# Half of the filter taps by DMA transpose through DRAM, half by TensorE per 128 channels, and a new instruction order, in a one-core kernel of a long convolution and an MLP mixer

## The chip, the cores and the metric

The kernel runs on one core of one Trainium2 chip. The metric is the device time of one execution in microseconds (us), lower is better; the time before is the median of three runs. A profile is one execution taken by the hardware profiler; its span is measured from the first to the last instruction that it shows.

## The reference

All tensors are bf16, with S = 2048 rows and D = 640 channels; the MLP is F = 1536 wide.

```python
x = A_q
g = sigmoid((x * gate_w).sum(-1, keepdims=True))
# branch a: depthwise shift, product with v, long convolution along S
k_shift = sum over t of 4 of k[s - t] * shift_k[:, t]
kv = k_shift * v
y  = irfft(rfft(pad(kv)) * rfft(pad(ssm_k)))[:S] + kv * ssm_D
a  = q * y
# branch b: a mixer block
h  = gelu(layernorm(x) @ w1); four groups of 160 channels shifted by 1, -1, 2, -2 rows
x1 = x + shifted(h) @ w2
b  = x1 + gelu(layernorm(x1) @ w3) @ w4
return g * a + (1 - g) * b
```

`ssm_k` has the shape (640, 2048): one filter of 2048 taps for each channel. The convolution wants the taps with time on the partitions, so the kernel has to transpose it. `ssm_D` is added to tap 0, which does the `kv * ssm_D` term.

## The kernel before, in words

Everything lives in one SBUF tensor, `arena`, and PSUM is used as four pairs of banks. Row s of a sequence is kept at partition p, block c and remainder rho with s = 1024c + 8p + rho, so that there are 8 values of rho and 2 of c.

The Python code doesn't issue instructions; it describes nodes. A node has an engine, a list of instructions, the memory that it reads and writes, an estimated cost and a tag. `Prog.schedule` (L181) and `_forward` (L200) then place the nodes one by one: at each step it takes the node that can start first by the estimates, and the table `PRIO` (L443 on) breaks ties by tag. What comes out is a fixed order for each of the five queues: PE (TensorE), ACT (ScalarE), DVE (VectorE), POOL (GpSimd) and SP, which issues most DMAs. Every engine runs its own list strictly in that order and waits on semaphores where `assign_waits` found a dependence. So the estimates and ranks decide the order, and a node that waits holds up all that stands behind it on its engine.

The work, in stages that overlap:

- Loads on SP (`load`, L664), one on ACT, and the identity matrix on POOL: x (= A_q) in steps of two rho and one c of 320 KB, w1, `shift_k`, ssm_k as five loads of 512 KB, k with its three halo rows, v, w2, the table `FM` (cF, 896 KB, for the forward transform) and `gate_w`.
- While nothing is there to work on, TensorE runs filler matmuls of ones (`fill`, L717), 35 nodes of five.
- LN1 (`bn`, L800; `ln_finish` on POOL, L794; `normal` on DVE, L626): statistics and normalisation of x, transposed on TensorE (L839) and evicted by ACT into `XT`.
- mm1 (L876) with GELU in the eviction; the 32-channel rests of the four groups go to their places by 18 small POOL DMAs (`tail`, L916).
- The taps (L762 to 782): 80 transposes of 128 by 128 on TensorE (L773), ten to a PSUM pair, and eight ACT evictions of 1280 columns (L779) into `TAP[p, h, t, d]`, where h is the half of 320 channels. DVE adds D to the row of tap 0.
- kv on DVE (`tt`, L621): the shift, the product with v.
- mm2 (L983) with the residual put in by an ACT seed (L966); LN2 by sums from ACT (L638) and a power on POOL; DMA transposes of SBUF to SBUF on SP (L1006) into `XT`.
- mm3 (L1026), mm4 (L1044), weights loaded by POOL.
- The convolution, per half of 320 channels: `forward` of taps ("h") and kv ("k") as matmuls (L1075), per half two `unit`s on DVE (butterflies, pointwise products, folds; all L621), the `inverse` matmuls (L1198), and the end `fin` on DVE with 16 output DMAs (L1227).

In `forward`, the first matmuls of kap 0 read the first 2048 columns of `FM` (`FM0`), those of kap 1 the other 1536 (`FM1`, `FM2`).

```python
forward("h", 0, "s3", "s4")
forward("k", 0, "s2", "t0")
unit(0, 0, ...); unit(0, 1, ...)
forward("h", 1, "s3", "s4")
forward("k", 1, "k0", "t1")
inverse(0, ...)
unit(1, 0, ...); unit(1, 1, ...)
inverse(1, ...)
```

Of the kernel before, what the change touches and what calls it, by code (L numbers as in the profile page):

```python
# [88 lines left out]
class Prog:  # L89
# [110 lines left out]
    def _forward(self):  # L200
# [38 lines left out]
        while left:  # L239
# [42 lines left out]
            if n.array:  # L282
                w = int((t - self.PHASE) // self.WINDOW)
                while window < w:
                    warm = duty > (0.42 if warm else 0.75) * self.WINDOW
                    window += 1
                    duty, carry = carry, 0.0
                if not warm:
# [14 lines left out]
            elif n.kind == "side":  # L303
                slink = max(slink, t + 1.0) + 0.2
                n.end = slink + (4.0 if link > t else 1.0)
            else:
                xlink = max(xlink, t + 1.0, link) + 1.2
# [115 lines left out]
def _bf16_bits(a):  # L423
# [5 lines left out]
FILL = 35  # L429
KV_DMA = ()  # L430
PW_DMA = ()
LN1_GROUPS = ((0,), (1,), (2, 3), (4, 5), (6, 7))
# [3 lines left out]
LN1_ACT = ()  # L436
INV = (0, 4, 2, 6, 1, 5, 3, 7)
FIN2 = (0,)
# [72 lines left out]
def bass_gated_mix__ssm_conv_h3__mixer_s_mlp__prompt_kernel(  # L511
# [66 lines left out]
    SSM = V(oS + 3 * SLOT, 10240).rearrange("p (c t) -> p c t", c=5)  # L578
    SHK = V(oGM + 1024, 2560).rearrange("p (j d) -> p j d", j=4)
    SHKROW = AR[0:1, oHT:oHT + 2560]  # L580
# [4 lines left out]
    DROW = AR[0:1, oS + 14080:oS + 14720]  # L585
# [93 lines left out]
    for sc in range(4):  # L679
        P.stage = sc  # L680
        for c in range(2):
            load("act" if sc == 0 and c == 1 else "sp", X[:, c, 2 * sc:2 * sc + 2, :], rows(A_q, c)[:, 2 * sc:2 * sc + 2, :],
                 128 * 2560, tag="x")
    P.stage = ""
    load("pool", ident.bitcast(U16), cI.ap(), 32768, tag="ident", cost=0.6)
    load("sp", w1v, B_w1.rearrange("(c p) f -> p c f", p=128), 819200, tag="w1")
# [3 lines left out]
    for c in range(2):  # L690
        P.stage = c
        if c == 0:
            for a, b in ((1, 113), (113, 128)):
                o = AR[a:b, oS:oS + 1920]
                load("sp", o, dram(A_k, (8 * a - 3) * D, [[8 * D, b - a], [1, 3 * D]]), (b - a) * 3840, tag="kh", group="halo")
        else:
            load("sp", KH[1][:, 0:3, :], dram(A_k, (1024 - 3) * D, [[8 * D, 128], [D, 3], [1, D]]), 128 * 3840, tag="kh")
        for h in range(2):
            P.stage = 2 * c + h
            load("sp", KH[c][:, 3 + 4 * h:7 + 4 * h, :], rows(A_k, c)[:, 4 * h:4 * h + 4, :], 128 * 5120, tag="k")  # L700
            load("sp", KV[:, 8 * c + 4 * h:8 * c + 4 * h + 4, :], rows(A_v, c)[:, 4 * h:4 * h + 4, :], 128 * 5120, tag="v")
    P.stage = ""
    for j in range(4):
        load("sp", w2v[:, j, :], B_w2[160 * j:160 * j + 128, :], 163840, tag="w2")
    for j in range(4):
        load("sp", w2v[32 * j:32 * j + 32, 4, :], B_w2[160 * j + 128:160 * j + 160, :], 40960, tag="w2", group="w2t")
# [3 lines left out]
    load("sp", DROW, A_ssm_D.rearrange("(o n) -> o n", o=1), 1280, tag="ssm")  # L710
    P.dma("sp", lambda e, ps: e.dma_start(GWT, gate_w.rearrange("(c p) -> p c", p=128), allow_slow_non_contiguous=True),
          w=[GWT], nbytes=400000, tag="gw")
# [3 lines left out]
    for _ in range(FILL):  # L716
        P.pe([(lambda e, ps: e.matmul(bank(ps, 0, 128), ones, ones, start=True, stop=True)) for _ in range(5)], r=[ones],  # L717
             cols=128 * 5, tag="fill", bits=(False, None))
# [47 lines left out]
    for m in range(8):  # L766
        P.stage = m // 4
        fns = []
        for i in range(2):
            t = 2 * m + i  # L770
            a, rho = t // 8, t % 8
            for c in range(5):
                fns.append(lambda e, ps, i=i, a=a, rho=rho, c=c: e.transpose(  # L773
                    half16(ps)[:, 1024 * i + 128 * c:1024 * i + 128 * c + 128],
# [502 lines left out]
```

## Time and profile before

| | |
|---|---|
| median of 3 runs | 236.66 us (236.05 to 238.21) |
| the profiled execution | 235.83 us, span 234.0 us |
| PE busy | 226.6 us, 97% of the span |
| DVE busy | 217.2 us, 93% |
| ACT busy | 175.6 us, 75% |
| POOL busy | 29.0 us, 12% |
| DMA | 27.69 MB in 26484 packets, 12657 of them under 512 B |

The profiled execution's time is 1.83 us longer than its span, and 0.83 us under the median. PE counts as busy while a matmul waits in its pipeline, so its share says little by itself: the spacing of a long run of equal matmuls tells whether it is dense. `L621` is the line of the helper that all DVE tensor-tensor operations share, and `L652` that of most ACT evictions; they are told apart by their shapes.

### The profile page before, as it was taken

The numbers are of one execution on the slowest core, as the hardware profiler recorded it, in microseconds if no ns is written. First come the engines' busy times: TensorE is split into PE (matmuls) and PEld (weight loads), VectorE is DVE, ScalarE is ACT, GpSimd is POOL, SyncE is SP. The second block draws the span as 40 slices with busy tenths as digits, with TensorE's granted clock in tenths as the row PEclk, the third lists the DMA queues.
The fourth block names the chain that finished last, engine by engine and source line by source line (L and its number), as shares of the span: only waits on it lengthen the run. The fifth ranks groups of instructions, "written<-read, shape, count | busy, mean of one in ns | idle before, by whom it ended". The sixth has DMA issues, their size and how long they took to land.

```text
span 234.0 us, 4160 instructions
## 1 busy us (share of the span) xinstructions
PE 226.6 (97%) x1689; PEld 147.4 (63%) x1689; DVE 217.2 (93%) x277; ACT 175.6 (75%) x287; POOL 29.0 (12%) x38
## 2 busy tenths in 40 slices
PE   7999998997999998999999998999999999999998
PEld 7799565554677755446764454457755764577777
DVE  3994799999999969998998999999999999999995
ACT  2458998999899999899959869889237224662683
POOL 1312530304003420005203000000000000000000
PEclk9889999999999999999999999999999999999999
DMA  7999999201005997000426500008008010001055
GB/s 222 385 408 315 349 398 331 74 0 27 0 0 192 344 339 95 0 0 3 84 44 102 112 0 0 3 9 216 3 0 224 3 56 0 0 3 56 0 172 169
DMA packets 26484, 27.69 MB, mean 118 GB/s; under 512 B 12657, under 2 KB 22258, under 8 KB 26338
## 3 DMA queue, kind: packets, MB, share of 16 engines
q1 hardware_dynamic: 24674, 21.57, 31.7%
q0 software_dynamic: 1648, 5.54, 6.9%
q10 hardware_dynamic: 144, 0.33, 0.7%
q8 instruction: 13, 0.21, 0.4%
q14 instruction: 5, 0.04, 0.1%
HBM read 21.66 MB, written 2.62 MB: 104 GB/s over the span
## 4 chain that ended last, share of the span: by engine, by line
PE 42%; ACT 18%; DVE 18%; SPq 7%; issue 6%; DMA 5%; POOL 2%; POOLq 1%; ACTq 0%; DVEq 0%
DVE arena L621 18%; PE PS L1044 17%; ACT arena L652 14%; PE PS L1026 9%; PE PS L1198 7%; SPq L664 7%; DMA arena<-in_A_k_dram 5%; PE PS L1075 3%; ACT PS L966 3%; POOL arena L794 2%; PE PS L983 2%; PE PS L717 2%; PE PS L876 1%; ACT arena L638 1%; POOLq L1247 1%
## 5 line engine op out<-in xcount | busy, mean ns | idle before, releaser
L621 DVE TENSOR_TENSOR arena<-arena 128x2560 bf16<-128x2560 bf16 (+5 forms) x181 | 193.4, 1127 | 4.0 <-DMA arena<-in_A_k_dram 1.6
L652 ACT ACTIVATE arena<-PS 128x640 bf16<-128x640 f32 (+5 forms) x136 | 97.8, 799 | 25.8 <-PE PS L1026 13.1
L1026 PE MATMUL PS<-arena 128*128 128x512 bf16 x240 | 52.8, 379 | 0.7 <-DMA arena<-arena 0.7
L1044 PE MATMUL PS<-arena 128*128 128x320 bf16 x384 | 52.8, 299 | 0.0
L1044 PEld LDWEIGHTS PS<-arena 128*128 128x128 bf16 x384 | 37.5, 98 | 14.9 <-issue 0.3
L652 ACT ACTIVATE arena<-PS,arena 128x320 bf16<-128x320 f32 (+1 forms) x48 | 27.9, 618 | 25.1 <-PE PS L1044 23.2
L1026 PEld LDWEIGHTS PS<-arena 128*128 128x128 bf16 x240 | 23.3, 98 | 28.4 <-issue 0.9
L1075 PE MATMUL PS<-arena 128*128 128x320 bf16 x224 | 34.2, 300 | 1.6 <-ACT arena L652 1.5
L1075 PEld LDWEIGHTS PS<-arena 128*128 128x128 bf16 x224 | 20.0, 98 | 14.7 <-ACT arena L652 6.2
L638 ACT ACTIVATE arena<-arena 128x640 bf16<-128x640 bf16 (+2 forms) x30 | 22.8, 786 | 2.8 <-DVE arena L824 2.7
L876 PE MATMUL PS<-arena 128*128 128x512 bf16 (+1 forms) x125 | 23.3, 337 | 0.4 <-ACT arena L779 0.2
L983 PE MATMUL PS<-arena 128*128 128x320 bf16 x160 | 22.2, 299 | 1.4 <-issue 1.4
L966 ACT ACTIVATE PS<-arena 128x640 f32<-128x640 bf16 x32 | 22.3, 718 | 0.1
L983 PEld LDWEIGHTS PS<-arena 128*128 128x128 bf16 x160 | 15.6, 98 | 7.7 <-issue 1.7
L794 POOL TENSOR_TENSOR arena<-arena 128x4 f32<-128x4 f32 (+1 forms) x9 | 13.6, 1514 | 54.0 <-DVE arena L621 37.9
L800 DVE BATCH_NORM_STATS2 arena<-arena 128x6 f32<-128x320 bf16 x32 | 13.7, 462 | 4.5 <-DMA arena<-in_A_q_dram 4.5
L1198 PE MATMUL PS<-arena 128*128 128x320 bf16 x128 | 17.9, 299 | 0.0
L876 PEld LDWEIGHTS PS<-arena 128*128 128x128 bf16 x125 | 11.7, 98 | 8.9 <-ACT arena L779 0.5
L717 PE MATMUL PS<-arena 128*128 128x128 bf16 x175 | 14.3, 256 | 1.5 <-DVE arena L674 1.5
L1198 PEld LDWEIGHTS PS<-arena 128*128 128x128 bf16 x128 | 12.5, 98 | 5.0
L717 PEld LDWEIGHTS PS<-arena 128*128 128x128 bf16 x175 | 13.4, 119 | 2.3 <-DVE arena L674 1.5
L626 DVE TENSOR_SCALAR arena<-arena 128x640 bf16<-128x640 bf16 (+3 forms) x35 | 10.3, 320 | 2.8 <-POOL arena L794 2.1
(31 smaller groups left out, 69.4 us busy)
## 6 DMA issues: line engine op xcount, KB each, us to landing
arena<-in_B_w_dram POOLq DMA_DIRECT2D x4, 960.0 KB, 8.1
arena<-in_A_v_dram SPq DMA_DIRECT2D x4, 640.0 KB, 13.5
arena<-in_A_ssm_k_dram SPq DMA_DIRECT2D x5, 512.0 KB, 11.4
arena<-in_A_k_dram SPq DMA_DIRECT2D x4, 640.0 KB, 16.2
arena<-in_A_q_dram SPq DMA_DIRECT2D x4, 640.0 KB, 4.9
out_dram<-arena SPq DMA_DIRECT2D x16, 160.0 KB, 2.0
arena<-in_A_q_dram SPq DMA_DIRECT2D x7, 320.0 KB, 7.8
arena<-cG POOLq DMA_DIRECT2D x1, 1024.0 KB, 5.0
```

Source lines behind the costliest of these rows:

```text
L621: return dve(lambda e: e.tensor_tensor(o, a, b, op), [a, b], [o], c_tt(n), tag=tag, **kw)
L638: node = P.op("act", lambda e, ps: e.activation(o, i, func, **kw), r=r, w=[o], cost=c_act(n, naps, acc is not None, psum=False), tag=tag, ...
L652: node = P.op("act", lambda e, ps: e.activation(ov, inner(ps), func, **kw), r=r, w=[o], cost=c_act(n, len(r), acc is not None), job=job, t ...
L717: P.pe([(lambda e, ps: e.matmul(bank(ps, 0, 128), ones, ones, start=True, stop=True)) for _ in range(5)], r=[ones], cols=128 * 5, tag="fil ...
L794: P.op("pool", lambda e, ps: e.tensor_tensor(r, v, hv, ALU.pow), r=[v, HALF], w=[r], cost=1.1, tag="ln")
L876: fns.append(lambda e, ps, b=b, c=c, lhsT=lhsT: e.matmul(bank(ps, b, 256 * n), lhsT, XT[:, c, r0:r0 + n, :], start=(c == 0), stop=(c == 4)))
L966: P.seed(job, lambda e, ps: e.activation(two(ps, 320), x, ACTF.Copy), [X[:, c, rho, :]], c_act(640, psum=False), tag)
L983: fns.append(lambda e, ps, hh=hh, ft=ft, lhsT=lhsT: e.matmul(bank(ps, hh, 320), lhsT, w2v[:, ft, 320 * hh:320 * hh + 320], start=False, st ...
L1026: fns.append(lambda e, ps, b=b, ft=ft, c=c, sc=sc: e.matmul(bank(ps, b, 512), w3v[:, c, 128 * ft:128 * ft + 128], XT[:, c, 2 * sc:2 * sc + ...
L1044: fns.append(lambda e, ps, hh=hh, ft=ft, lhsT=lhsT: e.matmul(bank(ps, hh, 320), lhsT, w4v[:, ft, 320 * hh:320 * hh + 320], start=False, st ...
L1075: fns.append(lambda e, ps, w=w, b=b, rhs=rhs, st=(first and n == 0), en=(n == len(ss) - 1): e.matmul(bank(ps, b, 320), w, rhs, start=st, s ...
L1198: fns.append(lambda e, ps, kap=kap, ri=ri, c=c, r=r, s=s, n=n: e.matmul(bank(ps, c, 320), GM[:, kap, ri, r, s, :], Qs[kap][:, r, ri, c, :] ...
```

## The change

1. The taps of channels 0 to 319 (h = 0): three nodes in place of eight. Each transposes one block of 128 channels (the last one 64) for all 16 groups of taps and is evicted as one ACT instruction of 2048 (1024) columns. Only 320 channels of `ssm_k` are loaded for it, as three loads.
2. The taps of channels 320 to 639 (h = 1): six DMA transposes on SP read `ssm_k` from DRAM and write `TAP[:, 1]` with the taps in natural order; each half of 1024 taps is then written to a DRAM tensor and read back in the 8p + rho order. Nothing on PE, ACT or DVE is left for this half.
3. D is added by two POOL instructions of 320 elements in place of one DVE instruction of 640.
4. x is loaded by rho singly for rho 0 and 1 (160 KB each), then in pairs as before. `FM` is split into two loads, 2048 and 1536 columns.
5. 60 filler nodes of one matmul in place of 35 of five.
6. The LN2 statistics are the same in fewer steps: the mean as such is worked out for one group alone.
7. The planner's estimates (bytes of loads, DMA transposes, side DMAs, POOL's power) and all ranks in `PRIO` are new, and so is the order of every queue. Switches for other variants (`FIN_DMA`, `LN1_STAT`) are off.

In the order that comes out, SP issues x rho 0 and 1, the first ssm_k block, shift_k, w1, x rho 2 and 3, the second block, the rest of x, one k load, D, the halo, v, the last ssm_k block, gate_w, v, the first part of `FM`, k with its halo, w2, v, v, then the six DMA transposes, then the second part of `FM`, the two writes to DRAM and the two reads back, and then the LN2 transposes. TensorE's list begins with 55 fillers and the eight matmuls of shift_k; in the `forward` of the first taps the first matmul that needs the second part of `FM` comes just ahead of the last mm1 block and of mm2. POOL's second D addition stands ahead of the last of the 18 `tail` DMAs.

The diff, without `PRIO` and the estimates:

```diff
-FILL = 35
+FILL = 60
+FILLN = 1
+X_LOADS = ((0, 1), (1, 2), (2, 4), (4, 6), (6, 8))
-    SSM = V(oS + 3 * SLOT, 10240).rearrange("p (c t) -> p c t", c=5)
+    SSM = V(oS + 3 * SLOT, 6144).rearrange("p (c t) -> p c t", c=3)
...
-    load("sp", V(oFM, 3584).bitcast(U16), cF.ap(), 128 * 7168, tag="FM")
-    for c in range(5):
-        load("sp", SSM[:, c, :], A_ssm_k[128 * c:128 * c + 128, :], 128 * 4096, tag="ssm")
+    for i, (a, b) in enumerate(((0, 2048), (2048, 3584))):
+        P.stage = i
+        load("sp", V(oFM + a, b - a).bitcast(U16), cF.ap()[:, a:b], (b - a) * 300, tag="FM")
+    for c in range(3):
+        P.stage = c
+        n = 128 if c < 2 else 64
+        load("sp", SSM[0:n, c, :], A_ssm_k[128 * c:128 * c + n, :], 5300 * n, tag="ssm")
...
-    for m in range(8):
...
-        job = P.pe(fns, r=[SSM[...], ident], cols=1400, tag="tap", bits=(False, False))
-        o = TAP[:, :, 2 * m:2 * m + 2, :].rearrange("p h t d -> p t h d")
-        P.op("act", ... ACTF.Copy), w=[o], cost=c_act(1280), job=job, tag="tap")
-    tt(t0row, t0row, DROW.rearrange("p (h d) -> p h d", h=2), ALU.add, 640, tag="ssmD")
+    for c in range(3):
+        n = 128 if c < 2 else 64
+        fns = [(lambda e, ps, c=c, n=n, t=t: e.transpose(
+            half16(ps)[:, n * t:n * t + n], SSM[0:n, c, 1024 * (t // 8) + t % 8:1024 * (t // 8) + 1024:8],
+            ident[0:n, 0:n])) for t in range(16)]
+        job = P.pe(fns, ...)
+        o = TAP[:, 0, :, 128 * c:128 * c + n]
+        evict(job, o, ..., ACTF.Copy, 16 * n, tag="tap")
+    def add_d(h):
+        t0row = TAP[0:1, h, 0, :]
+        P.op("pool", lambda e, ps: e.tensor_tensor(t0row, t0row, DROW[h], ALU.add), ...)
+    add_d(0)
+    back = nc.dram_tensor("taps1", (2048, 320), BF16).ap()
+    for a in range(2):
+        o = TAP[:, 1, 8 * a:8 * a + 8, :]
+        for d in (0, 128, 256):
+            n = min(128, 320 - d)
+            P.dma("sp", ... e.dma_start_transpose(o[:, :, d:d + n], A_ssm_k[320 + d:320 + d + n, 1024 * a:1024 * a + 1024]))
+        if a == 0:
+            add_d(1)
+        half = back[1024 * a:1024 * a + 1024, :]
+        out_ = P.dma("sp", ... e.dma_start(half.rearrange("(q p) d -> p q d", p=128), o), tag="tW")
+        in_ = P.dma("sp", ... e.dma_start(o, half.rearrange("(p r) d -> p r d", r=8)), tag="tR")
+        in_.deps.add(out_)
...
     def sum_group(rhos):
-        ts(mean, s1, 1.0 / D, None, ALU.mult, None, 4, tag="ln")
-        tt(t, mean, mean, ALU.mult, 4, tag="ln")
-        ts(v, s2, 1.0 / D, 1e-5, ALU.mult, ALU.add, 4, tag="ln")
-        tt(v, v, t, ALU.subtract, 4, tag="ln")
+        tt(t, s1, s1, ALU.mult, 4, tag="ln")
+        dve(lambda e: e.scalar_tensor_tensor(out=v, in0=t, scalar=-1.0 / D, in1=s2, op0=ALU.mult, op1=ALU.add), ...)
+        ts(v, v, 1.0 / D, 1e-5, ALU.mult, ALU.add, 4, tag="ln")
```

More of the change, by code (lines that the diff above doesn't have):

```diff
@@ L304, in _forward @@
                 slink = max(slink, t + 1.0) + 0.2
-                n.end = slink + (4.0 if link > t else 1.0)
+                n.end = slink + (5.0 if link > t else 2.6)
             else:
-                xlink = max(xlink, t + 1.0, link) + 1.2
+                xlink = max(xlink, t + 1.0, link) + n.bytes / 136.5e3
                 n.end = xlink + 0.5
@@ L677, in bass_gated_mix__ssm_conv_h3__mixer_s_mlp__prompt_kernel @@
     act(JUNK[:, 0:1], ones[:, 0:1], ACTF.Gelu_apprx_tanh, 1, tag="warm")
-    for sc in range(4):
-        P.stage = sc
+    for a, b in X_LOADS:
+        P.stage = a
         for c in range(2):
-            load("act" if sc == 0 and c == 1 else "sp", X[:, c, 2 * sc:2 * sc + 2, :], rows(A_q, c)[:, 2 * sc:2 * sc + 2, :],
-                 128 * 2560, tag="x")
+            load("act" if a == 0 and c == 1 else "sp", X[:, c, a:b, :], rows(A_q, c)[:, a:b, :], 163840 * (b - a), tag="x")
     P.stage = ""
     load("pool", ident.bitcast(U16), cI.ap(), 32768, tag="ident", cost=0.6)
-    load("sp", w1v, B_w1.rearrange("(c p) f -> p c f", p=128), 819200, tag="w1")
+    load("sp", w1v, B_w1.rearrange("(c p) f -> p c f", p=128), 890000, tag="w1")
     load("sp", SHKROW, dram(A_shift_k, 0, [[2560, 1], [1, 2560]]), 5120, tag="shk")
@@ L711, in bass_gated_mix__ssm_conv_h3__mixer_s_mlp__prompt_kernel @@
+    P.stage = ""
+    for h in range(2):
+        load("sp", DROW[h], A_ssm_D.rearrange("(o n) -> o n", o=2)[h:h + 1, :], 1280, tag="D")
     P.dma("sp", lambda e, ps: e.dma_start(GWT, gate_w.rearrange("(c p) -> p c", p=128), allow_slow_non_contiguous=True),
-          w=[GWT], nbytes=400000, tag="gw")
+          w=[GWT], nbytes=140000, tag="gw")
     for _ in range(FILL):
-        P.pe([(lambda e, ps: e.matmul(bank(ps, 0, 128), ones, ones, start=True, stop=True)) for _ in range(5)], r=[ones],
-             cols=128 * 5, tag="fill", bits=(False, None))
+        P.pe([(lambda e, ps: e.matmul(bank(ps, 0, 128), ones, ones, start=True, stop=True)) for _ in range(FILLN)], r=[ones],
+             cols=128 * FILLN, tag="fill", bits=(False, None))
@@ new lines, in act_stats @@
+    def act_stats(rho):
+        rsl = slice(rho, rho + 1)
+        for c in range(2):
+            x = X[:, c, rho, :]
+            act(JUNK, x, ACTF.Copy, 640, scale=1.0 / D, acc=MV1[:, rho, 2 * c:2 * c + 1], accgroup=("m1", rho), tag="st")
+            act(JUNK, x, ACTF.Square, 640, scale=D ** -0.5, acc=MV1[:, rho, 2 * c + 1:2 * c + 2], accgroup=("m1", rho),
+                tag="st")
+        m, s, v = MV1[:, rsl, 0:4:2], MV1[:, rsl, 1:4:2], VAR1[:, rsl, 0:2]
+        dve(lambda e: e.scalar_tensor_tensor(out=v, in0=m, scalar=-1.0, in1=m, op0=ALU.mult, op1=ALU.mult),
+            [m], [v], 0.08, tag="ln")
+        dve(lambda e: e.scalar_tensor_tensor(out=v, in0=v, scalar=1e-5, in1=s, op0=ALU.add, op1=ALU.add),
+            [v, s], [v], 0.08, tag="ln")
+        ln_finish(VAR1, RS1, 0.75, rsl)
@@ L1209, in inverse @@
                 evict(job, o, lambda ps, c=c: bank(ps, c, 320), ACTF.Copy, 320, scale=GG[:, gi:gi + 1], tag="gy")
[L1210 to L1211 removed]
+            paired = INV.index(rho) // 2 < FIN2[half]
+            pair = rho // 4 == 1 and paired
+            if paired and not pair:
                 continue
@@ L1221, in inverse @@
             n = 1280 if pair else 640
-            tt(g2, g2, Qh[:, :, sel, :], ALU.mult, n, tag="fin")
-            tt(xs, xs, g2, ALU.add, n, tag="fin")
+            if half in FIN_DMA:
+                qs = Qh[:, :, sel, :]
+                tt(qs, g2, qs, ALU.mult, n, tag="fin")
+                P.dma("pool", lambda e, ps, xs=xs, qs=qs: e.dma_start(xs, qs, accum_op=ALU.add), r=[xs, qs], w=[xs],
+                      nbytes=256 * n, cost=0.9, kind="acc", tag="fina")
+            else:
+                tt(g2, g2, Qh[:, :, sel, :], ALU.mult, n, tag="fin")
+                tt(xs, xs, g2, ALU.add, n, tag="fin")
             for r1 in range(sel.start, sel.stop, 4):
```

85 lines of the change are left out of this document (46 added, 39 removed), and 50 rows, old and new, of the table PRIO.

## The prediction

> **What bounds the kernel now.** I read the busy time by stage first, then the chain of waits, then the timelines of DVE, PE and SP at the places that the change touches. The windows show that no engine alone is the bound:
>
> ```profile
> 0.00:29.24 29.24, 27.78 (x274) 22.95 (x275) 20.59 (x74) 17.69 (x22) 8.87 (x16) 0.94 0.97 336
> 13.37:86.81 73.44, 70.11 (x636) 48.57 (x634) 66.13 (x87) 69.52 (x119) 19.13 (x27) 1.00 0.61 209
> 29.24:221.80 192.56, 187.54 (x1296) 115.40 (x1295) 187.46 (x185) 150.30 (x250) 20.13 (x22) 1.00 0.30 82
> ```
>
> Columns after the length: busy time of PE, weight load, DVE, ACT, POOL, then granted clock, DMA share and GB/s. Until 29.24 us DMA is the full one (share 0.97), and DVE works 20.59 of 29.24 us. From 29.24 to 221.80 DVE works 187.46 of 192.56 us: it idles 5.1 us. ACT, from its first LN1 eviction to 86.81, works 69.52 of 73.44 us. The chain passes through all of them:
>
> ```profile
> 17.45 11.66 DMA arena<-in_A_k_dram
> ...
> 80.09 6.72 ACT arena L652 x12
> ...
> 94.57 11.21 DVE arena L621 x8
> ...
> 217.53 11.95 PE PS L1198 x88
> 229.48 3.63 PE PS L717 x65
> ```
>
> It goes from the load of k (landed at 29.11) to ACT until about 87 us, DVE to about 145, then PE. The 65 fillers at the end fill time in which the last results are evicted, multiplied and written out, so dropping them gives nothing. PE is dense where it counts: equal matmuls follow each other at 13.20/96 = 0.1375 us and 17.43/80 = 0.218 us.
>
> ```profile
> 9.95 2.32 PE L717 MATMUL PS<-arena 128*128 128x128 bf16 x20
> 12.06 1.27 PE L839 MATMUL PS<-arena 128*128 128x128 bf16 x10
> 13.13 1.11 PE L717 MATMUL PS<-arena 128*128 128x128 bf16 x15
> 14.91 4.53 PE L876 MATMUL PS<-arena 128*128 128x256 bf16 x40
> 21.49 2.70 PE L773 MATMUL PS<-arena 128*128 128x128 bf16 x40
> 58.73 1.52 PE L983 MATMUL PS<-arena 128*128 128x320 bf16 x10 [1.41 <-issue]
> 120.93 17.43 PE L1026 MATMUL PS<-arena 128*128 128x512 bf16 x80
> 158.81 13.20 PE L1044 MATMUL PS<-arena 128*128 128x320 bf16 x96
> ```
>
> So a gain must come on all three engines at once: an earlier start and less work on DVE, ACT and PE. I cost each, and the end follows the one that gains least.
>
> **DVE.** What the loads make DVE wait for:
>
> ```profile
> 5.10 1.28 DVE L800 BATCH_NORM_STATS2 arena<-arena 128x6 f32<-128x320 bf16 x3 [2.69 <-DMA arena<-in_A_q_dram]
> 9.98 0.75 DVE L626 TENSOR_SCALAR arena<-arena 128x640 bf16<-128x640 bf16 x2
> 20.23 1.36 DVE L626 TENSOR_SCALAR arena<-arena 128x640 bf16<-128x640 bf16 x3 [1.20 <-POOL arena L794]
> 23.37 1.45 DVE L800 BATCH_NORM_STATS2 arena<-arena 128x6 f32<-128x320 bf16 x3 [1.78 <-DMA arena<-in_A_q_dram]
> 29.24 4.23 DVE L621 TENSOR_TENSOR arena<-arena 128x5120 bf16<-128x5120 bf16 x2 [1.57 <-DMA arena<-in_A_k_dram]
> ```
>
> The first statistics wait for 320 KB loads; with 160 KB I take 0.9 us less (bounds: 0, and 2.1, since a 160 KB output lands 2.0 us after its issue, which began at 0.74 for x). By their place in SP's order the last x load has 4.4 MB up to its end and the first k with its halo 5.6 MB; DMA moved 0.336 MB per us up to 29.24, which is 13 and 17 us, and even 5 us late that is before DVE asks (about 18 and 24.5 us). So the waits of 1.78 and 1.57 go. Rho 2 and 3 may be late next: 2.6 MB by some 9 to 10.5 us, asked for at about 10: I charge 0.5. The 1.20 for POOL has one 5120 multiply (2.8 us) as its cover in the new order; I count half of it. Sum: 0.9 + 1.78 + 1.57 + 0.6 - 0.5 = 4.3 us earlier. The work shrinks a little:
>
> ```profile
> L621 DVE TENSOR_TENSOR arena<-arena 128x4 f32<-128x4 f32 x8 | 1.2, 156 | 0.0
> L621 DVE TENSOR_TENSOR arena<-arena 1x640 bf16<-1x640 bf16 x1 | 0.5, 473 | 0.0
> L779 ACT ACTIVATE arena<-PS 128x1280 bf16<-128x1280 bf16 x8 | 9.4, 1284 | 0.0
> L652 ACT ACTIVATE arena<-PS 128x640 bf16<-128x640 f32 x84 | 53.8, 737 | 6.8 <-PE PS L723 5.7 <-PE PS L983 0.8 <-DVE arena L621 0.3
> ```
>
> The D row (0.47) moves to POOL, and LN2 loses three of its small operations (3 x 0.16). DVE together: 4.3 + 0.5 + 0.5 = 5.3 us.
>
> **ACT.** Eight evictions of 1284 ns, 10.3 us one by one, become three with 2048 + 2048 + 1024 columns. At 1284/1280 ns a column that is 5.1 us, so 5.2 us less (9.4 busy, with overlap, gives 4.3; I take 4.6).
>
> ```profile
> 13.37 1.24 ACT L652 ACTIVATE arena<-PS 128x1280 bf16<-128x1280 bf16 x1 [2.53 <-PE PS L839]
> ```
>
> Its first LN1 eviction at 13.37 waited for the first LN1 transposes. These stood behind 20 fillers of 2.32 us, although DVE began their inputs at 9.98. In the new order the eight shift_k matmuls come right before them, all 55 early fillers being over by then, and DVE is 0.9 us early: I take 10.0 for the transposes in place of 12.06, and 2 us for ACT. ACT together 6.6 us.
>
> **PE.** The start gives 2.0. Of 80 tap transposes 48 are left, at 2.70/40 us: 32 x 0.0675 = 2.2 (the 16 narrow ones counted in full). Of the 20 fillers after 12.06 (15 took 1.11, five more the same each) five are left: 1.1. The 1.41 us at 58.73, where mm2 waited after POOL had issued its last five tails at 54.80, goes, because those tails come with the mm1 block some 7 us earlier and mm2 follows at once only for the groups that are ready; I count all of it, bound 0. Together 6.7 us, if nothing new stands in the way.
>
> **The new wait.** The second part of `FM` is issued behind six DMA transposes, and TensorE, in order, stops at the first matmul that reads it, ahead of the last mm1 block and all of mm2.
>
> ```profile
> 112.00:118.00 6.00, 6.00 (x46) 4.33 (x45) 6.00 (x8) 5.70 (x10) 1.57 (x1) 1.00 0.55 109
> 0.00:35.00 35.00, 33.38 (x328) 26.63 (x328) 26.34 (x78) 23.45 (x28) 11.20 (x20) 0.95 0.98 346
> L1006 SPq DMA_TRANSPOSE arena<-arena x16: 1200/1276/1836, 84.2 to 132.1; - x16
> DMA to landing us min/median/max: 2.6/2.7/6.3
> 23.18 10.33 SPq L664 DMA_DIRECT2D arena<-in_A_v_dram  x1
> out_dram<-arena SPq DMA_DIRECT2D x16, 160.0 KB, 2.0
> 54.80 2.60 POOL L916 DMA_DIRECT2D arena<-arena  x5 [11.45 <-ACT arena L652]
> ```
>
> When it lands: 12.3 MB of loads stand before the transposes, and DMA had moved 346 x 35 = 12.1 MB by 35 us, so they have the DMA from 35.5. The six move 1.31 MB, from DRAM, which no row shows. The nearest is the four LN2 transposes in 112 to 118: 109 GB/s at a share of 0.55, or 198 GB/s if the share were full: 6.6 us. Lower end, the rate of the plain loads: 3.8 us. Upper end, SP's issue: 1.276 us for 160 KB is 128 GB/s, 10.2 us, if SP can't run ahead; that its last load took 10.33 us to issue says that it is held up by what is under way. I take 6.6, the same kind of transfer. Then 0.39 MB of `FM`, 1.1 us, and 2.0 us to land: 45.2 (42.4 to 48.8).
>
> When PE asks: 65 mm1 matmuls at 0.218 (14.2), 50 at 4.53/40 (5.7), 80 + 48 transposes (8.6), 32 forward matmuls at 0.1375 (4.4), gates under 1: 33.7 us after 10.0, so 43.7. The wait is 1.5 us (0 to 5.1). Behind it stand the last mm1, mm2, ACT's seeds and evictions of both. PE: 6.7 - 1.5 = 5.2; ACT: 6.6 - 1.5 = 5.1; DVE 5.3, untouched, since its built order holds nothing but kv and small LN2 operations there.
>
> [...]
>
> **What costs nothing.** The write to DRAM and back of the second half's taps has no row; it ends by some 55 us even at twice the transposes' time, and `forward` of that half comes after the first units' butterflies have freed its slots, near 100 us. SP has nothing else to issue until the LN2 transposes (84.2 before). POOL's second D addition waits for the first three transposes (39 to 43 us) and holds up the last tail DMA, wanted at 47 or later; if they came after 47, mm2 would wait for them one for one. The read of `gate_w` comes earlier in the queue, as do the gate matmuls.
>
> Fewer fillers could leave the clock low. The row shows one stretch already:
>
> ```profile
> 10.00:12.00 2.00, 2.00 (x21) 2.00 (x21) 2.00 (x10) 0.84 (x2) 1.12 (x2) 0.50 1.04 397
> 12.00:14.00 2.00, 2.00 (x27) 2.00 (x26) 2.00 (x8) 0.63 (x1) 0.00 (x0) 0.66 1.03 414
> ```
>
> It stood at 0.50 in 10 to 12 and rose within 12 to 14, with fillers running beside. The built order has real work from 10 us; I count no difference, and up to 1.7 us of loss if another 3.4 us run at half. [...]
>
> **Sum.** The least gain is ACT's 5.1, the others are 5.2 and 5.3: 5.2 us. The profiled run 235.83 becomes 230.6, its span 228.8. The median stands 0.83 above the profiled run, so I predict 236.66 - 5.2 = 231.5. Its own range is 229 to 234, from the start (0 to 2.1) and the wait.
>
> **The rivals.** (1) The wait doesn't arise: transposes at the plain rate land `FM` at 42.4, before PE asks. PE and ACT then gain 6.6, DVE 5.3 is the bound but for its start (up to 1.2 more): 6.5 us, 230.2. For it: DMA is otherwise empty then. Against: the row of 109 GB/s. (2) The gain is used up later: in the new order the 56 forward matmuls of kv's first half follow mm2 as one block, with 16 evictions of 737 ns, 11.8 us, against 7.7 us of matmuls. TensorE, dense before, would lose 4.1 us: 235.6, no change. Against: 72 of them (24, 16 and 32) together with gates took the same 12 us before (79.39 to 91.39), so part of that is paid already:
>
> ```profile
> 79.39 3.73 PE L1075 MATMUL PS<-arena 128*128 128x320 bf16 x24 [0.38 <-ACT arena L652]
> 86.86 4.53 PE L1075 MATMUL PS<-arena 128*128 128x320 bf16 x32
> ```
>
> (3) Slower: the transposes from DRAM are much slower than those in SBUF. PE's and ACT's gain without the wait is 6.6, so `FM` must land after 43.7 + 6.6 = 50.3 to make it a loss, and after 52.7 for 1%: the transposes would need 14 us, 94 GB/s. At half of the issue rate, 64 GB/s, they take 20.5, `FM` lands at 59.1, the wait is 15.4: 236.66 - 6.6 + 15.4 = 245.5. For it: one of the LN2 transposes took 6.3 us to land. Against: share 0.55 at 109 GB/s.
>
> **Chances.** Forecast 0.46, rival 1 0.20, rival 2 0.16, rival 3 0.18. Within 1% (234.3 to 239.0, about what a measurement can tell from no change) is rival 2: 0.16; faster is the first two: 0.66; slower 0.18. The range for 8 in 10 goes from rival 1 with the better start, 228, to 238, which leaves out most of rival 3.
>
> **What would show it.** Right: first LN1 transposes near 10 us; first 5120 multiply on DVE near 25 without a wait for k; three tap evictions of 2.0, 2.0 and 1.0 us; a stop of TensorE of 0 to 5 us near 44 that ends with the load of cF; mm2 dense from about 47; every stage after that some 5 us earlier. Wrong: tap evictions over 2.5 us, TensorE waiting for cF past 50 us, DVE idle over 5 us in the kv and unit stage, or a clock below 1.00 after 15 us.

## The result and the profile after

| | before | after |
|---|---|---|
| median | 236.36 us (235.77 to 238.21, four executions) | 245.88 us (243.37 to 246.64, four) |
| ratio after/before | | 1.0371, 95% interval 1.0276 to 1.0465 |
| profiled execution, span | 235.83, 234.0 us | 243.37, 241.6 us |
| mean granted clock | | 0.967 |

The change made the kernel 3.7% slower; 2.2% faster was predicted. Medians here and below are of all executions, while each ratio compares only the fast executions with those of the kernel before run beside them (whose medians are 236.36 to 236.89), and among the profiles only that of e4 is of a slow execution. The profiled execution is the fastest of the four, so what follows shows the loss at its smallest. In spans, 228.8 us was predicted and 241.6 came: 12.8 us to be explained.

The chain that ended last, in the profile of the kernel after, in the part where the change acts (start, length, what; shown from 33.64 us on, without the pieces of 0.04 or 0.05 us called "issue"):

```profile
33.64 2.19 PE PS L1126 x16
35.83 0.68 SPq L805
36.55 4.48 SPq L805
41.08 1.28 SPq L805
42.39 2.21 SPq L805
44.64 1.31 SPq L805
45.99 1.27 SPq L805
47.31 3.81 DMA arena<-cF
51.16 2.31 PE PS L1126 x8
...
83.45 12.68 DMA arena<-arena
96.38 12.40 PE PS L1077 x50
```

Before, the chain passed this stretch mostly through ACT. Now it leaves the engines twice. From 35.83 to 51.1 us it is SP issuing the transposes (L805) one after the other and then the load of cF; and from 83.45 to 96.13 it is one LN2 transpose (arena to arena), on which mm3 (L1077) waits.

TensorE's timeline (start, length, what, in brackets the wait ahead of it and what ended it):

```profile
9.91 0.73 PE L883 MATMUL PS<-arena 128*128 128x128 bf16 x10
42.12 2.34 PE L1126 MATMUL PS<-arena 128*128 128x320 bf16 x16
51.16 2.31 PE L1126 MATMUL PS<-arena 128*128 128x320 bf16 x8 [6.70 <-DMA arena<-cF]
53.27 3.15 PE L923 MATMUL PS<-arena 128*128 128x512 bf16 x10
56.26 4.24 PE L1030 MATMUL PS<-arena 128*128 128x320 bf16 x30
96.38 14.55 PE L1077 MATMUL PS<-arena 128*128 128x512 bf16 x60 [4.39 <-DMA arena<-arena]
```

The first LN1 transposes are early, as forecast. Then there are two stops: 6.70 us for cF, and 4.39 us ahead of mm3, for which the kernel before has this row:

```profile
92.44 13.11 PE L1026 MATMUL PS<-arena 128*128 128x512 bf16 x60 [0.72 <-DMA arena<-arena]
```

So mm3 starts 3.94 us later than before, and its 60 matmuls take 1.44 us more. Clock and DMA by stage in the kernel after (columns as in the prediction's first fence):

```profile
0.00:35.00 35.00, 31.69 (x318) 24.40 (x319) 30.28 (x84) 24.57 (x30) 14.49 (x21) 0.95 0.98 317
48.00:55.00 7.00, 3.84 (x13) 1.83 (x14) 6.97 (x3) 3.08 (x6) 0.92 (x2) 0.51 1.00 276
96.00:103.00 7.00, 6.62 (x25) 2.70 (x26) 1.70 (x6) 2.80 (x6) 0.00 (x0) 0.76 0.01 2
```

Each stop brings a stretch at a low clock, 0.51 and 0.76. DMA moved 317 GB/s in the first 35 us, 346 before.

SP's timeline shows why cF is late, and the source row gives the duration of a transpose's issue (minimum, median, maximum):

```profile
28.15 0.90 SPq L670 DMA_DIRECT2D arena<-in_A_v_dram  x2
29.10 18.17 SPq L805 DMA_TRANSPOSE arena<-in_A_ssm_k_dram  x6
47.31 0.58 SPq L670 DMA_DIRECT2D arena<-cF  x1
...
L805 SPq DMA_TRANSPOSE arena<-in_A_ssm_k_dram x6: 1272/1759/7407, 29.1 to 46.0; - x6
```

The six transposes take SP 18.17 us, and cF is issued only at 47.31. The chain above has their issues one by one: the first, from 29.10, took 7.41 us and the second 4.48; the other four took 1.27 to 2.21. The second ended at 41.03, and the last load ahead of the six, the last part of v, landed at 41.2 (issued at 28.62, 12.6 us to landing).

On POOL, the weights of the second half of the kernel now come behind the LN2 power (L824):

```profile
72.69 3.62 POOL L824 TENSOR_TENSOR arena<-arena 128x4 f32<-128x4 f32 x1 [23.77 <-DVE arena L632]
76.28 0.63 POOL L670 DMA_DIRECT2D arena<-cG  x1
79.83 1.70 POOL L670 DMA_DIRECT2D arena<-in_B_w_dram  x2 [2.92 <-DVE arena L627]
83.14 1.74 POOL L670 DMA_DIRECT2D arena<-in_B_w_dram  x2 [1.62 <-PE PS L1030]
```

In the kernel before they came ahead of it:

```profile
71.36 0.58 POOL L664 DMA_DIRECT2D arena<-cG  x1 [13.96 <-DVE arena L621]
73.91 1.67 POOL L664 DMA_DIRECT2D arena<-in_B_w_dram  x2 [1.97 <-DVE arena L626]
78.21 1.75 POOL L664 DMA_DIRECT2D arena<-in_B_w_dram  x2 [2.64 <-PE PS L983]
81.25 2.34 POOL L794 TENSOR_TENSOR arena<-arena 128x4 f32<-128x4 f32 x1 [1.29 <-DVE arena L621]
```

cG is 1 MB, w4 (issued second) and w3 (third) are 2 MB each: 5 MB, issued between 76.28 and 84.9. The four first LN2 transposes, which follow the power, are issued by SP in that same stretch, from 76.8 on. In the kernel before, they were issued from 84.2 on, behind all weights, of which the last landed at 88.6. Time from issue to landing of all 16 LN2 transposes (minimum, median, maximum), kernel after:

```profile
L1057 SPq DMA_TRANSPOSE arena<-arena x16: 1198/1276/2967, 76.8 to 143.6; - x16
DMA to landing us min/median/max: 2.6/2.7/14.0
```

The maximum was 6.3 us before and is 14.0 now, with the same median. Of the first four, the third and the fourth are the late ones: they landed at 95.7 and 96.1, just as the last part of the weights did (95.8).

### The profile page after: what moved, and what is told of

Read it like the earlier page. It is cut to its first block, busy times and chain, and to the rows that moved or that the text cites. A ratio compares the mean times of both kernels' runs of the same rounds, so it can differ in the third digit from the quotient of the medians.

```text
span 241.6 us, 3874 instructions
## 1 busy us (share of the span) xinstructions
PE 220.4 (91%) x1542; PEld 138.0 (57%) x1542; DVE 217.8 (90%) x273; ACT 170.9 (71%) x282; POOL 33.8 (14%) x40
## 4 chain that ended last, share of the span: by engine, by line
PE 68%; ACT 10%; DMA 9%; SPq 5%; DVE 4%; POOL 2%; issue 1%; ACTq 0%
PE PS L1095 22%; PE PS L1077 21%; PE PS L1249 7%; ACT arena L658 7%; PE PS L923 6%; DMA arena<-arena 5%; PE PS L1126 5%; SPq L805 5%; DVE arena L627 3%; DMA arena<-in_A_shift_k_dram 2%; PE PS L883 2%; ACT arena L644 2%; PE PS L1030 2%; DMA arena<-cF 2%; PE PS L780 2%; ACT PS L1013 2%
## 5 line engine op out<-in xcount | busy, mean ns | idle before, releaser
L627 DVE TENSOR_TENSOR arena<-arena 128x2560 bf16<-128x2560 bf16 (+4 forms) x176 | 194.0, 1160 | 10.1 <-ACT arena L658 8.8
L658 ACT ACTIVATE arena<-PS 128x640 bf16<-128x640 f32 (+5 forms) x139 | 102.7, 821 | 40.8 <-PE PS L1077 20.8
L1077 PE MATMUL PS<-arena 128*128 128x512 bf16 x240 | 54.5, 386 | 4.4 <-DMA arena<-arena 4.4
L1095 PE MATMUL PS<-arena 128*128 128x320 bf16 x384 | 53.6, 299 | 0.0
L1095 PEld LDWEIGHTS PS<-arena 128*128 128x128 bf16 x384 | 37.5, 98 | 15.0 <-issue 0.2
L1126 PE MATMUL PS<-arena 128*128 128x320 bf16 x224 | 35.7, 306 | 8.3 <-DMA arena<-cF 6.7
L1077 PEld LDWEIGHTS PS<-arena 128*128 128x128 bf16 x240 | 23.5, 99 | 33.3 <-issue 7.0
L1126 PEld LDWEIGHTS PS<-arena 128*128 128x128 bf16 x224 | 20.4, 99 | 22.4 <-DMA arena<-cF 7.0
L824 POOL TENSOR_TENSOR arena<-arena 128x4 f32<-128x4 f32 (+1 forms) x9 | 15.3, 1702 | 79.8 <-DVE arena L632 79.6
L923 PE MATMUL PS<-arena 128*128 128x512 bf16 (+1 forms) x125 | 23.9, 346 | 0.3 <-ACT arena L658 0.3
L1030 PE MATMUL PS<-arena 128*128 128x320 bf16 x160 | 23.1, 299 | 0.4 <-ACT PS L1013 0.4
L1030 PEld LDWEIGHTS PS<-arena 128*128 128x128 bf16 x160 | 15.1, 98 | 7.0 <-ACT PS L1013 1.2
L1249 PE MATMUL PS<-arena 128*128 128x320 bf16 x128 | 18.2, 299 | 0.2 <-ACT arena L658 0.2
L923 PEld LDWEIGHTS PS<-arena 128*128 128x128 bf16 x125 | 12.4, 101 | 9.7 <-issue 1.1
L1249 PEld LDWEIGHTS PS<-arena 128*128 128x128 bf16 x128 | 12.4, 98 | 5.5 <-issue 0.5
L963 POOL DMA_DIRECT2D arena<-arena x18 | 9.8, 550 | 13.7 <-ACT arena L658 13.7
L632 DVE TENSOR_SCALAR arena<-arena 128x640 bf16<-128x640 bf16 (+3 forms) x32 | 9.8, 338 | 2.0 <-PE PS L923 1.0
L728 PE MATMUL PS<-arena 128*128 128x128 bf16 x60 | 5.2, 266 | 1.1 <-DVE arena L680 1.1
```

Of the source, the lines that this page charges most:

```text
L627: return dve(lambda e: e.tensor_tensor(o, a, b, op), [a, b], [o], c_tt(n), tag=tag, **kw)
L658: node = P.op("act", lambda e, ps: e.activation(ov, inner(ps), func, **kw), r=r, w=[o], cost=c_act(n, len(r), acc is not None), job=job, t ...
L824: P.op("pool", lambda e, ps: e.tensor_tensor(r, v, hv, ALU.pow), r=[v, HALF], w=[r], cost=cost, tag="ln")
L923: fns.append(lambda e, ps, b=b, c=c, lhsT=lhsT: e.matmul(bank(ps, b, 256 * n), lhsT, XT[:, c, r0:r0 + n, :], start=(c == 0), stop=(c == 4)))
L1030: fns.append(lambda e, ps, hh=hh, ft=ft, lhsT=lhsT: e.matmul(bank(ps, hh, 320), lhsT, w2v[:, ft, 320 * hh:320 * hh + 320], start=False, st ...
L1077: fns.append(lambda e, ps, b=b, ft=ft, c=c, sc=sc: e.matmul(bank(ps, b, 512), w3v[:, c, 128 * ft:128 * ft + 128], XT[:, c, 2 * sc:2 * sc + ...
```

## The experiments

Three theories follow from the traces. A: the late cF is the whole loss, what follows is its echo. B: there is a second fault of its own, the weights moving beside the LN2 transposes. C: what costs is the low clock after a stop, more than the stop. Within A there are two: SP is held because the loads issued earlier are still under way (A1), or the transposes that read DRAM are slow (A2, the prediction's third rival).

The experiments are edits of the order that the planner has made, right after `P.schedule()`; the code that describes the work stays as it is but for e4. `_before(nodes, mark)` and `_after(nodes, mark)` take nodes out of their queue's list and put them next to `mark`; all other queues keep their order. All kernels are the kernel after with the edit named; the ratios are against the kernel before. e1, e3 and e5 to e8 test places and queues, e2 the clock, and e4 whether it matters that the six are transposes.

| | median, us | ratio (95% interval) | span | wait for cF | mm3: start, its wait |
|---|---|---|---|---|---|
| before | 236.36 | | 234.0 | | 92.44, 0.72 |
| after | 245.88 | 1.0371 (1.0276 to 1.0465) | 241.6 | 6.70 | 96.38, 4.39 |
| e1 cF ahead of the transposes | 237.68 | 1.0006 (0.9969 to 1.0044) | 233.2 | none | 87.83, 3.34 |
| e2 TensorE kept busy ahead of cF | 246.21 | 1.0378 (1.0305 to 1.0450) | 241.6 | 0.48 | 95.00, 4.00 |
| e3 e1, transposes after all loads | 236.26 | 0.9988 (0.9947 to 1.0029) | 233.4 | 0.79 | 88.21, 3.58 |
| e4 plain copies for the transposes | 245.76 | 1.0347 (1.0277 to 1.0417) | 245.2 | 8.25 | 98.91, 5.77 |
| e5 e1, POOL: w3, w4, cG | 233.46 | 0.9831 (0.9777 to 0.9885) | 229.4 | none | 85.70, 1.12 |
| e5b the same again | 232.77 | 0.9811 (0.9757 to 0.9865) | 229.4 | 0.41 | 85.93, 1.08 |
| e6 POOL: w3, w4, cG alone | 240.75 | 1.0160 (1.0107 to 1.0212) | 239.0 | 9.19 | 95.30, 0.81 |
| e7 e1, POOL: w4, w3, cG | 240.37 | 1.0144 (1.0084 to 1.0205) | 237.2 | 0.94 | 92.27, 6.35 |
| e8 e1, POOL: cG, w3, w4 | 232.66 | 0.9805 (0.9764 to 0.9845) | 230.2 | none | 86.80, 1.43 |

### e1: the second part of FM ahead of the transposes

```diff
+    sp = P.order["sp"]
+    tts = [n for n in sp if n.tag.startswith("tT:")]
+    _before(_pos(sp, "FM:1"), tts[0])
```

> One edit to the changed kernel: SP issues the load of the second part of FM ahead of the six DMA transposes; every other place in every queue is kept. Theory A (one wait does it): TensorE's wait of 6.70 us for cF at 44.5 goes, mm2 starts near 47 in place of 56.3, the low clock around 48 to 55 goes with it (some 2 us), DVE's wait of 6.57 us for ACT at 59.5 and the wait of mm3 at 92 to 96.4 shrink to under 1 us each; the time is 229 to 234, ratio to the kernel before 0.97 to 0.99. Rival B (the new order has a second fault of its own: the weights of mm3 and mm4 stand on POOL behind the LN2 power and move at the same time as the LN2 transposes, and mm3 waits for both): the first wait goes, but mm3 still waits over 3 us and the time is 238 to 242, ratio 1.005 to 1.025.

TensorE's timeline in e1:

```profile
48.39 4.24 PE L1030 MATMUL PS<-arena 128*128 128x320 bf16 x30 [0.25 <-ACT PS L1013]
...
87.83 14.80 PE L1077 MATMUL PS<-arena 128*128 128x512 bf16 x60 [3.34 <-DMA arena<-arena]
```

There is no wait for cF, and mm2 starts at 48.39, 7.9 us earlier than after. The span falls by 8.4 us, and the ratio falls to 1.0006, no difference from before. So the first stop is worth 8 us; but mm3 still waits 3.34 us, its 60 matmuls take 14.80 us, and the kernel is not faster than before. That ratio lies between what A had forecast (0.97 to 0.99) and what B had (1.005 to 1.025). A as the whole story is excluded, B is not.

### e2: the clock alone

The node of four matmuls just ahead of the wait is repeated, so that TensorE works through the wait.

```diff
+    hold = pe[pe.index(_pos(pe, "fwdh:1")[0]) - 1]
+    hold.fns = hold.fns * 12
```

> The changed kernel with the wait for cF left in, but TensorE kept busy in it: the node that stands last before the wait repeats its four matmuls eleven times more (44 of 0.1375 us, 6.0 us; each repeat starts its sum anew, so the result is the same). If the low clock of 48 to 55 us is a price of the wait by itself (theory C), the clock stays at 1.00 there, the eight forward matmuls after it take 1.2 us in place of 2.31 and the mm1 block of ten 2.2 in place of 3.15, and the time falls by 1.5 to 3 us against the changed kernel, to a ratio of about 1.025 to 1.03. If the wait alone matters (theory A without the clock), the time stays within 1 us of the changed kernel, ratio about 1.037.

In e2, the windows of the two low stretches and the rows of TensorE behind each stop:

```profile
48.00:55.00 7.00, 6.52 (x42) 3.81 (x41) 6.97 (x4) 3.36 (x6) 1.75 (x2) 1.00 1.04 285
95.00:103.00 8.00, 8.00 (x24) 3.04 (x25) 2.42 (x8) 3.17 (x6) 0.00 (x0) 0.63 0.01 2
```

```profile
51.86 1.26 PE L1126 MATMUL PS<-arena 128*128 128x320 bf16 x8 [0.48 <-DMA arena<-cF]
95.00 16.00 PE L1077 MATMUL PS<-arena 128*128 128x512 bf16 x60 [4.00 <-DMA arena<-arena]
```

The clock at cF is full and the eight matmuls take 1.26 us in place of 2.31. That brings mm3 1.4 us forward (95.00 for 96.38), and then its 60 matmuls take 16.00 us for 14.55, since the second low stretch is deeper (0.63). The time is the same as that of the kernel after. C falls as the cause of the loss: a full clock behind the first stop gained nothing at the end, because the second stop stayed and its low stretch took back the 1.4 us. What the low clock of the second stop costs, e2 does not test; e5 shows it below.

### e3: the transposes held back until the loads are done

As e1, and the first transpose waits for the last load of v; POOL's second D addition goes behind the last tail, which it would otherwise hold up.

```diff
+    _before(_pos(sp, "FM:1"), tts[0])
+    tts[0].deps.add([n for n in sp if n.tag.startswith("v:")][-1])
+    _after([_pos(pool, "ssmD:0")[-1]], [n for n in pool if n.tag.startswith("tail:")][-1])
```

> As e1, and besides the first of the six DMA transposes waits until the last load of v has landed, and POOL's second D addition stands behind the last tail DMA. The transposes then meet an empty queue. Theory A1 (they are slow to issue because the loads ahead fill the queue): each of the six issues in 1.2 to 2.1 us, 8 to 11 us in all in place of 18.2, and lands within 4 us of its issue. Theory A2 (a transpose that reads DRAM is slow by itself): the issues still take over 15 us in all. Time: under theory A the same as e1 within 1 us, since the taps are needed only near 100 us; under B 238 to 242.

The same transposes, in e3:

```profile
L805 SPq DMA_TRANSPOSE arena<-in_A_ssm_k_dram x6: 1272/1302/1394, 43.9 to 50.7; - x6
...
DMA to landing us min/median/max: 2.9/3.7/4.4
```

Behind finished loads the longest issue is 1.39 us, not 7.41, the six take 8.1 us of SP (43.89 to 52.0), and each lands 2.9 to 4.4 us after its issue. So what held SP for 18.17 us was the loads ahead, and not reading DRAM: A1, not A2. The other runs agree: in the kernel after the issue of the second transpose ended at 41.03, 0.2 us before the last load ahead of it landed, and in e1 and e2 the longest issue took 7.85 and 7.84 us.

### e4: plain copies in their place

```diff
-            ... A_ssm_k[320 + d:320 + d + n, 1024 * a:1024 * a + 1024]: e.dma_start_transpose(o, i)
+            ... A_v[0, 1024 * a:1024 * a + 1024, d:d + n].rearrange("(q p) d -> p q d", p=128): e.dma_start(o, i)
```

> The changed kernel with the order as it is, but the six transposes are plain copies of as many bytes with the same pieces of 256 B (rows of v in place of the second half's taps, so the second half of the convolution is computed with other taps; the amount of work is the same). Theory A2 (the transpose is what is slow): the six issue in under 6 us, FM lands before 44 us, TensorE's wait is under 1 us and the time is that of e1. Theory A1 (whatever stands there is held by the full queue, and the small pieces cost what they cost): the issues still take over 12 us, and the wait is 3 to 7 us.

SP's row and TensorE's stop in e4:

```profile
L805 SPq DMA_DIRECT2D arena<-in_A_v_dram x6: 1513/1610/6089, 30.6 to 46.4; - x6
```

```profile
51.98 2.32 PE L1126 MATMUL PS<-arena 128*128 128x320 bf16 x8 [8.25 <-DMA arena<-cF]
```

In e4 rows of v stand in for the second half's taps, as many bytes, written in pieces of up to 256 B (the second half is then convolved with other numbers). These plain copies hold SP for 17.3 us, with one issue of 6.09, and TensorE waits 8.25 us. So it does not matter that the six are transposes, and A2 fails a second time. That anything at all would hold SP there is not shown: the second part of FM, in larger pieces, took 1.44 us to issue at that place in e1. Behind loads that still ran the six held SP for 17.3 us as plain copies and for 18.17 as transposes; behind finished loads the 1.31 MB of transposes took 8.1 us of issue in e3, 162 GB/s, and plain copies were not tried there.

### e5, e5b and e6: the weights in another order

e5 is e1 with POOL's three weight loads in the order w3, w4, cG. w3 can be issued only when mm2 has ended, and POOL is in order, so all three now start behind three of the first four LN2 transposes (the fourth, issued at 76.04, comes 0.3 us after w3).

```diff
+    pool = P.order["pool"]
+    w3, w4, gm = _pos(pool, "w3"), _pos(pool, "w4"), _pos(pool, "GM")
+    _after(w4 + gm, w3[-1])
```

> As e1 (the second part of FM ahead of the transposes), and POOL issues the loads in the order w3, w4, cG in place of cG, w4, w3, behind the same LN2 power. In e1 the DMA moved 5 MB of weights from 69 to 88 us; the four LN2 transposes of the first group stood in it, the last for 11.3 us, mm3 waited 3.34 us, its 60 matmuls took 14.80 in place of 13.1 at a low clock, and DVE then waited 3.72 us for ACT. Theory B (that collision is the second fault): mm3 waits under 1 us, its 60 matmuls take about 13.1, DVE's wait falls under 1 us, and the end comes 4 to 5 us earlier than in e1: 231 to 233, ratio to the kernel before 0.975 to 0.985. Rival D (what is left is set by TensorE's or DVE's order after mm3's start, so the time saved at mm3 comes back as a wait later): mm3 starts earlier but the time stays within 1 us of e1, ratio 0.995 to 1.003.

POOL, the landing of the LN2 transposes and TensorE, in e5:

```profile
75.72 3.47 POOL L670 DMA_DIRECT2D arena<-in_B_w_dram  x4 [6.80 <-PE PS L1030]
79.18 0.56 POOL L670 DMA_DIRECT2D arena<-cG  x1
```

```profile
DMA to landing us min/median/max: 2.6/2.7/9.4
```

```profile
85.70 13.11 PE L1077 MATMUL PS<-arena 128*128 128x512 bf16 x60 [1.12 <-ACT arena L658]
```

The transposes land at most 9.4 us after their issue (13.0 in e1), mm3 starts 2.1 us earlier than in e1 and waits 1.12 us for ACT, not for a DMA; its 60 matmuls take 13.11 us at full clock (1.00 in 85 to 92 us), 1.7 less than in e1. The span falls by 3.8 us, which is these 2.1 and 1.7: the low clock was nearly half of the price of this stop. This confirms B, and the kernel is now 1.7% faster than the one before. A repeat gave the same:

> The kernel of e5 again, on the same chip as e8, so that the two can be set beside each other: ratio 0.977 to 0.989 as before, mm3's first matmul at 85 to 86.5.

e6 makes the POOL edit alone and leaves the late cF.

> The changed kernel with POOL's loads in the order w3, w4, cG and the load of FM left where it was. Theory A plus B (two faults that add): TensorE still waits 6 to 7 us for cF at 44.5, but the wait of 4.39 us at mm3 and the low clock at 96 to 100 go, and the time is 239 to 242, ratio 1.01 to 1.025. Theory A alone: no difference from the changed kernel, ratio 1.03 to 1.04.

The wait for cF is there in full, 9.19 us, and the one at mm3 is gone (0.81 us, 13.11 us for the 60):

```profile
95.30 13.11 PE L1077 MATMUL PS<-arena 128*128 128x512 bf16 x60 [0.81 <-DMA arena<-arena]
```

So the two faults are separate, and they add: from 1.0371 the ratio falls by 0.021 with the POOL edit alone, by 0.037 with SP's alone and by 0.054 to 0.056 with both, against 0.058 for the sum. e6 has the order of the kernel after up to its wait for cF, so 6.70 and 9.19 us are two values of the same wait.

### e7 and e8: which of the weights it is

e7 moves only cG behind the weights (w4, w3, cG), e8 only w4 behind w3 (cG, w3, w4); both with e1's edit.

```diff
e7
+    _after(_pos(pool, "GM"), _pos(pool, "w3")[-1])
e8
+    _after(_pos(pool, "w4"), _pos(pool, "w3")[-1])
```

> As e1, and of POOL's loads only cG (1 MB, not needed before the inverse transform) is moved behind the weights: w4, w3, cG. Theory B: the transposes have 1 MB less ahead of them, some 2.8 us at 360 GB/s; mm3 waits 0.5 to 1.5 us, and the time lies between e1 and e5, 233 to 235. If the order among the loads doesn't matter (only that they are there): as e1.

> As e1, with POOL's loads in the order cG, w3, w4. e7 moved cG from the idle DMA of 69 to 72 us to behind the weights and mm3 then waited 6.35 us, more than e1's 3.34; e5 also held w4 back and mm3 waited 1.1. If what counts is how many bytes run beside the four transposes and w3 (theory B), cG goes back into the idle stretch, w4 stays behind w3, and mm3 starts at 84.5 to 86, as in e5 or up to 1 us earlier; the time is that of e5 or up to 1 us less, ratio 0.975 to 0.985. If it was cG's place that cost e7 its time and w4's place is indifferent, the same result as e5 would also come, but e1 (cG, w4, w3) should then not have waited; a ratio above 0.995 would say that cG ahead of the weights hurts, and e5's gain came from moving cG.

POOL and TensorE in e7:

```profile
73.74 1.71 POOL L670 DMA_DIRECT2D arena<-in_B_w_dram  x2 [3.51 <-DVE arena L627]
77.07 1.74 POOL L670 DMA_DIRECT2D arena<-in_B_w_dram  x2 [1.62 <-PE PS L1030]
78.81 0.55 POOL L670 DMA_DIRECT2D arena<-cG  x1
```

```profile
92.27 14.38 PE L1077 MATMUL PS<-arena 128*128 128x512 bf16 x60 [6.35 <-DMA arena<-arena]
```

and POOL in e8:

```profile
69.68 0.63 POOL L670 DMA_DIRECT2D arena<-cG  x1
76.17 3.52 POOL L670 DMA_DIRECT2D arena<-in_B_w_dram  x4 [5.86 <-PE PS L1030]
```

The forecast for e7, an improvement, was wrong: its ratio is 1.0144 and e1's 1.0006. The 360 GB/s in it are about what DMA moved: 359 in 90 to 95 us of the kernel after, 364 in 80 to 85 of e7. In e1 cG was issued at 68.78, half a microsecond ahead of the first transpose (69.32); in e7 it joins w4 and w3 beside them (the four transposes are issued from 70.73 to 80.76), mm3 waits 6.35 us, and a transpose took up to 14.6 us to land. Some of e7's loss is from before: its mm2 started at 50.18, 1.8 us after e1's. e8 keeps cG early and puts w4 behind w3, which waits for mm2's end at 76.17: 232.66 us, level with e5 and e5b within their intervals, with mm3 at 86.80 (84.5 to 86 was forecast). So with w4 behind w3 it makes no difference whether cG is early or last; what hurts in e1 and in the kernel after is w4, 2 MB issued some 3 us ahead of w3 in the middle of the LN2 transposes.

One rival is left, since w4 ahead of w3 also delays w3, which mm3 reads: mm3 might have waited for its weights. The trace of the kernel after settles it. mm3's first matmuls read the first half of w3 alone, and that landed at 92.7, 3.7 us before mm3 began; the last of the four transposes landed at 96.1, 0.2 us before. In e1 too the last of them landed 0.2 us before mm3 began, at 87.6.

## Why the prediction was wrong, step by step

**Where it was right.** The first LN1 transposes stood at 9.91 us (10.0 predicted). The first 5120 multiply on DVE came at 24.16 without a wait for k (near 25). The tap evictions were two of 1877 and one of 1018 ns (2.0, 2.0, 1.0). TensorE's last matmul ahead of cF ended at 42.12 + 2.34 = 44.46 (43.7). In the kernel after the taps came back from DRAM with nobody waiting for them, and the D additions on POOL were hidden. Of its own signs of being wrong, two came: TensorE waited for cF past 50 us, and the clock fell below 1.00 after 15 us.

**"The new wait" failed, in its term for the end of the loads.** The prediction had the 12.3 MB ahead of the transposes done at 35.5 us, from the 346 GB/s of the kernel before. In the kernel after DMA moved 317 GB/s in the first 35 us (11.1 MB, not 12.1), and the last of these loads landed at 41.2, 5.7 us later. The transposes are not the reason: in e3 they wait for it, and the first of them was issued only at 43.89. In the kernel after SP was held by its first two transposes until 0.2 us before these loads had landed (7.41 and 4.48 us, to 41.03).

The second term, 6.6 us for the six transposes, was too short as well: behind finished loads they took 8.1 us of SP (e3). That did not show, because two of the six were issued while the loads still ran. From the end of the loads to the landing of cF at 51.1 it is 9.9 us, for which the prediction had 6.6 + 1.1 + 2.0 = 9.7; that these agree is partly luck. The upper end of the range, 48.8, kept the 35.5 and so was too early too, although the row of a held issue was there, the last load of v that took 10.33 us.

So TensorE went on at 51.16 and not at 45.2, after a wait of 6.70 us where 1.5 was predicted and 5.1 was the most. With it came a loss that no term had: the 0 to 1.7 us for a low clock in "What costs nothing" were for the fillers at the start, half of another stretch like that of the kernel before, where the clock stood at 0.50 for 3.41 us (9.94 to 13.35), while here the clock was 0.51 behind the stop, by which the eight matmuls and the next ten of mm1 took 2.31 + 3.15 us where e2 (for the eight) and e1 (2.33 for the ten) have 1.26 + 2.33, so 1.9 more. Sum of this step: 6.0 later and 1.9 clock, 7.9 us. e1, which has no wait for cF at all and so lacks the predicted 1.5 us too, has a span 8.4 us shorter.

**A term was missing.** Nothing in the prediction looked at POOL's weights against the LN2 transposes. The change moved both; the order of POOL's list in the built kernel shows the power ahead of cG, w4 and w3, where before it came behind them. Everything ahead of mm3 was taken to move by the same 5 us. e5 shows 3.8 us of span for it. Whoever moves a step past another on a queue has to ask what transfers now run at the same time.

**The gain without a new wait was too high.** PE was to gain 6.7 us, and in e5, without the stops, mm3 starts 92.44 - 85.70 = 6.7 us earlier than before. That agreement is luck. 16 more of the forward matmuls stand behind the start of mm3 than before (112 for 96): 16 x 0.1375 = 2.2 us. From mm3's start to the end of the last inverse matmul the kernel before took 229.48 - 92.44 = 137.0 us, e5 139.2. That is the 2.2, counted in the traces and not tried by itself. With it, e5's gain is 6.7 - 2.2 = 4.5 us of span (measured: 234.0 - 229.4 = 4.6). e5 is the case of the first rival, in which the wait does not arise, and that was to gain 6.5.

**The second rival named the result of this, and not the mechanism.** It let the gain be used up in the 56 forward matmuls that follow mm2, 11.8 us for 7.7. In the kernel after they took 8.8 us (83.21 to 91.98). The 2.2 us went to the order of the list instead.

**The third rival had a time near the result, 245.5 for 245.88, by luck.** Its mechanism, slow transposes from DRAM, is excluded by e3 and e4; it had cF landing at 59.1 (51.1 measured), and by its own break-even of 50.3 a landing at 51.1 costs 0.8 us. The low clock, the weights and the 16 matmuls, which were not in it, account for most of the rest.

In spans, from 241.6 measured: e1 takes off 8.4 for cF with what it brings, e5 another 3.8 for the weights, and 229.4 is left, 0.6 above the 228.8 predicted. That closeness is no proof of the rest: the 228.8 include 1.5 us of wait that e5 does not have, and the 16 matmuls make up for it.

Open: why DMA moved less in the first 35 us than before (317 for 346 GB/s). What makes the wait for cF differ from one execution to the next (6.70 and 9.19 us with the same order up to it). How much of the gain in e5 the DMA transposes of the second half bring, and how much the three evictions and the earlier loads, was not tried; that would need another plan.

## What to carry to other kernels

Here transfers of small pieces, issued behind 12 MB of loads, held their issuing engine, SP, until these loads had landed (41.03 us, the last load at 41.2). So take the end of the loads from a landing and not from a mean rate, and put a load with a deadline ahead of the transfers that can wait. When a queue's order changes, list which transfers now run at the same time, and compare their deadlines: here 2 MB that nothing needed soon delayed small transposes that TensorE waited for, 4.39 us in the kernel after and 3.34 in e1. And when a count of saved work agrees with the start of a stage, as the 6.7 us did, see first that the same work stands ahead of it: 2.2 us of it had only moved behind.

## What the runs showed of the hardware that was not expected

- The issue of one DMA transpose held SP for 7.41 us behind 12 MB of loads that had not all landed (6.09 for a plain copy); behind finished loads the same issue took 1.27 to 1.39 us (e3). In the kernel after the second transpose's issue ended 0.2 us before the last load ahead of it landed (41.03 and 41.2 us).
- An LN2 transpose that lands in 2.7 us (median) took up to 14.0 us in the kernel after and 14.6 in e7 with 5 MB of POOL's weight loads under way. In the kernel after the two late ones, issued at 81.70 and 83.45, landed at 95.7 and 96.1, within 0.4 us of the last part of the weights (95.8), though that part was issued after them, at 84.02.
- After a stop of 6.70 us TensorE's clock was 0.51 in 48 to 55 us, which holds the end of the stop, after one of 4.39 us 0.76 in 96 to 103, and after one of 3.34 us in e1 0.79 in 87 to 95. Behind the stop of 1.12 us in e5 it was 1.00 in 85 to 92, and the 60 matmuls took 13.11 us there and behind the stop of 0.81 us in e6, as in the kernel before. From which length of a stop on the clock falls was not tried.
